# Lightning attention before a snake MLP: the product with the state in 64x64 tiles of four quadrants, in two passes

## The chip, the cores and the metric

One Trainium2 chip, one NeuronCore of it, one launch. The metric is the device time of the launch in microseconds. The kernel before took 213.11 us (median of 3 runs, 212.89 to 213.43). Engines are named as in the profile: PE is TensorE (its sequencer PEq), PEld its weight loads, DVE is VectorE, ACT is ScalarE, POOL is GpSimd, SP is SyncE, which here only issues DMAs.

## The reference, cut to what matters

Batch 4, 8 heads, 768 positions, head size 64; the attention goes in blocks of 64 positions with a running state of 64x64 a head. Its output, 3072 rows of 512, feeds an MLP with 2048 hidden columns.

```python
for b in range(nb):                                   # 12 blocks of 64 positions
    intra = einsum('bhic,bhjc->bhij', qb, kb) * Dmask # local scores, masked by decay
    intra = einsum('bhij,bhjd->bhid', intra, vb)
    inter = einsum('bhid,bhde->bhie', qb * lam_pow, kv_state)   # the product with the state
    out[:, :, sl] = intra + inter
    kv_state = lam_block * kv_state + einsum('bhsd,bhse->bhde', kb * rev_pow, vb)
h = x @ w_in                                          # x: out with the heads side by side
s = sin(alpha * h)
g = h + s * s / alpha
return g @ w_out
```

## The kernel before, in words

**Chunks and groups.** The 768 positions are cut into six chunks t of 128. A chunk of all four batches makes 512 rows of x, kept transposed in `xt[t]` (four blocks of 128 columns of the model, 512 rows), which is also a group g of the MLP. Everything is ordered by hand: the kernel's Python code writes the instructions in the order in which each engine runs them.

**The MLP.** A group has sixteen slots f. `hidden(g, f)` (L398) is four matmuls of 512 columns into a PSUM bank, then a sine on ScalarE (L405) and a square, on ScalarE (L408) or, for odd f of group 0, VectorE (L416). `finish(g, f)` (L413) on VectorE makes the column block of `gall` from the square and the bank, and so frees the bank. From group 1's fourth slot on, three banks go round, so `hidden(g, f)` needs `finish(g, f-3)`. `project(g, m, part)` (L422) is four matmuls of 512 columns, a quarter of an output tile; such units stand in a list `behind`, and `run(1)` takes the next. A unit with part 3 is followed by a copy out of PSUM (L434 on VectorE, L436 on ScalarE) and a store through SP. In slots that have a larger attention stage, `run` is skipped (L628).

**The attention of chunk g+1** is laid into the slots of group g. For chunks 2 to 5, in blocks of 64: `states` (L328, matmuls L331) makes the blocks' k-v products, `update` (L335 and `new_state` L306) adds them on VectorE to the decayed state (L313, four instructions for a pair of batches and a block) and GpSimd casts the state to BF16 into `SBD` (L317); `scores` (L342, matmuls L350) and `masks` (L354) make the masked local scores; `outputs` (L361) makes the product with the state (L368) and the local product (L376) into four banks, one for each pair of batches and block; `leave` (L382) scales the banks on VectorE into `xt`. Banks 4 to 7 serve states, scores and outputs one after the other. `slots(g)` (L582) puts states, scores and outputs into slots 7, 10 and 12 of group 1 and 4, 8 and 12 of the later groups. `feed(g)` (L599) places the loads of the next chunks (`pair_load`), the transposes of k and q by DMA (`turn_by_dma`, issued by SP) and GpSimd's decay of k (`pair_ready`).

Chunks 0 and 1 go in one block of 128 by `turns` (L227, transposes on TensorE, evicted by ScalarE), `scores1` (L268) and `outs` (L279, with the product with the state in L283 and the local one in L287), `states1` (L296). Chunk 0 is the prologue; chunk 1's transposes and scores stand in slots 12 to 15 of group 0 and behind it (L545 to L579).

**The product with the state.** Partitions hold two heads (hp, hd): head 2 hp in the lower 64, head 2 hp + 1 in the upper. `SBD` holds, for each batch and pair of heads, a 128x128 weight with the two 64x64 states on the diagonal and zeros beside them, so that one matmul over 128 rows gives both heads; x's blocks of 128 columns hold heads 2c and 2c+1. The zeros are written once: one buffer by VectorE (L146), two by GpSimd (L512). Each cast (L317) writes 64 partitions, so there are two of them for each update.

**Loads.** `load` (L101), `load_w_in` (L88, L93) and `load_w_out` (L96) are DMAs issued by GpSimd, in its program order between its own work. Eight can be in flight: each waits for the landing of the eighth before it.

Of the kernel before, what the change touches and what calls it, by code (L numbers as in the profile page):

```python
# [15 lines left out]
def kernel(  # L16
# [70 lines left out]
    def load_w_in(i):  # L87
        nc.gpsimd.dma_start(out=w_in_sb[i][:],  # L88
                            in_=moe_w_in[:, i * 512:(i + 1) * 512].rearrange("(c p) g -> p c g", p=P))

    def load_w_in0(n):
        w = slice(256 * n, 256 * n + 256)
        nc.gpsimd.dma_start(out=w_in_sb[0][:, :, w], in_=moe_w_in[:, w].rearrange("(c p) g -> p c g", p=P))  # L93
# [22 lines left out]
    load_w_in0(0)  # L116
    load_w_in0(1)
# [26 lines left out]
    SBD = [consts.tile([P, B, HP, 2, D], BF16, name=f"sbd{n}") for n in range(3)]  # L144
    S_of = [consts.tile([P, B, HP, D], FP32, name=f"S{n}") for n in range(2)]
    nc.vector.memset(SBD[1][:], 0.0)  # L146
# [12 lines left out]
    ln_hd = consts.tile([P, HP], FP32, name="ln_hd")  # L159
    for hd, half in enumerate(HALF):  # L160
        nc.vector.tensor_copy(out=ln_hd[half, :], in_=by_pair[half, hd, :])
# [8 lines left out]
    def decay_tables():  # L170
        later["R128"] = powers("R128", 2, lnlam[:], [P, H])
        later["NE64"] = powers("NE64", 3, by_pair, [P, 2, HP])
        later["R64"] = powers("R64", 4, lnlam[:], [P, H])
        nc.scalar.activation(out=L128[:], in_=ln_hd[:], func=ACTF.Exp, scale=float(T))
        nc.scalar.activation(out=L64[:], in_=ln_hd[:], func=ACTF.Exp, scale=float(D))

    def etab(*hps):
        for hp in hps:
            nc.scalar.activation(out=Etab[:, hp, :], in_=pos_row[:], func=ACTF.Exp, scale=ln_hd[:, hp:hp + 1])
# [15 lines left out]
    def home(t, blk):  # L195
        return SBD[2 if blk else t % 2]

# [80 lines left out]

    def outs(t, b, n, eng=None):  # L279
        O = bank("O_ps", n)[:].rearrange("p (c i) -> p c i", c=HP)  # L280
        if t:
            for hp in range(HP):
                nc.tensor.matmul(out=O[:, hp, :], lhsT=home(t, 0)[:, b, hp, :, :], rhs=QT[t][:, b, hp, :],  # L283
                                 start=(hp == 0), stop=False, skip_group_check=True)
        for hp in range(HP):
            for hd in range(2):
                nc.tensor.matmul(out=O[halves(hd), hp, :], lhsT=vn[t][:, b, 2 * hp + hd, :],  # L287
                                 rhs=STm[t, b][:, hd, hp, :], start=(t == 0 and hp == 0), stop=True,
# [17 lines left out]
    def new_state(n, pr, ps, decay, dst):  # L306
# [9 lines left out]
        for hd in range(2):  # L316
            nc.gpsimd.tensor_copy(out=dst[halves(hd), bs, :, hd, :], in_=S[halves(hd), bs, :, :])  # L317
# [42 lines left out]

    def outputs(t):  # L361
        O = {(pr, blk): bank("O_ps", AB[2 * pr + blk])[:].rearrange("p (u c i) -> p u c i", u=2, c=HP)
             for pr in range(2) for blk in range(2)}
        for pr in range(2):
            for blk in range(2):
                for u in range(2):
                    for hp in range(HP):
                        nc.tensor.matmul(out=O[pr, blk][:, u, hp, :], lhsT=home(t, blk)[:, 2 * pr + u, hp, :, :],  # L368
                                         rhs=QT[t][:, 2 * pr + u, hp, halves(blk)],
                                         start=(u == 0 and hp == 0), stop=False, skip_group_check=True)  # L370
        for pr in range(2):
            for u in range(2):
                for hp in range(HP):
                    for blk in range(2):
                        for hd in range(2):
                            nc.tensor.matmul(out=O[pr, blk][halves(hd), u, hp, :],  # L376
# [302 lines left out]
```

## Time and profile before

| | us |
|---|---|
| median of 3 runs (lowest, highest) | 213.11 (212.89, 213.43) |
| the profiled execution, in all | 213.7 |
| its span, first to last instruction | 211.9 |
| PE busy, matmuls | 201.8 |
| DVE busy | 136.6 |
| ACT busy | 141.4 |
| POOL busy | 99.4 |

How to read it: the span is one profiled execution's time from the first to the last instruction; the profiled execution as a whole took 1.8 us longer, for what lies around it. "Busy" is the time in which an engine had at least one instruction of its own running; matmuls overlap, so a matmul's duration is longer than the distance to the next. The distance of two starts in the timeline says what a group of matmuls costs TensorE. In a timeline row the first number is the start in us from the span's start, the second the length, then engine, line, operation, names and count; in brackets how long the engine stood idle before it and what ended that. In rows of groups, "x16 | 10.3, 684" is the count, the busy us and the mean ns of one. The granted clock of TensorE was 1.0 throughout.

### The profile page before, as it was taken

The numbers are of one execution on the slowest core, as the hardware profiler recorded it, in microseconds if no ns is written. First come the engines' busy times: TensorE is split into PE (matmuls) and PEld (weight loads), VectorE is DVE, ScalarE is ACT, GpSimd is POOL, SyncE is SP. The second block draws the span as 40 slices with busy tenths as digits, with TensorE's granted clock in tenths as the row PEclk, the third lists the DMA queues.
The fourth block names the chain that finished last, engine by engine and source line by source line (L and its number), as shares of the span: only waits on it lengthen the run. The fifth ranks groups of instructions, "written<-read, shape, count | busy, mean of one in ns | idle before, by whom it ended". The sixth has DMA issues, their size and how long they took to land.

```text
span 211.9 us, 4823 instructions
## 1 busy us (share of the span) xinstructions
PE 201.8 (95%) x1961; PEld 100.0 (47%) x1961; DVE 136.6 (64%) x258; ACT 141.4 (67%) x229; POOL 99.4 (47%) x104
## 2 busy tenths in 40 slices
PE   6679998999998999999999999999999999999993
PEld 2444444654444644446444446444446444444452
DVE  5675995774589888987649977648767544444000
ACT  4695988506895698764776765776774787887121
POOL 8999979985499995999003930004000000000000
PEclk9999999999999999999999999999999999999999
DMA  5999999999999999999999007711101101110212
GB/s 104 154 161 206 206 161 182 182 180 155 166 219 180 128 138 148 183 146 120 182 146 200 37 20 104 150 46 53 53 0 53 49 0 49 49 52 2 99 52 98
DMA packets 98759, 24.44 MB, mean 115 GB/s; under 512 B 90913, under 2 KB 95793, under 8 KB 98737
## 3 DMA queue, kind: packets, MB, share of 16 engines
q0 software_dynamic: 77040, 13.37, 85.0%
q1 hardware_dynamic: 20512, 10.50, 24.5%
q10 hardware_dynamic: 1184, 0.27, 0.6%
q8 instruction: 15, 0.25, 0.5%
q14 instruction: 8, 0.06, 0.1%
HBM read 27.28 MB, written 6.29 MB: 158 GB/s over the span
## 4 chain that ended last, share of the span: by engine, by line
PE 70%; DMA 10%; DVE 7%; ACT 5%; issue 3%; POOL 3%; DVEq 0%; ACTq 0%; POOLq 0%
PE ops L427 34%; PE hps L402 26%; DMA qn<-in_q_dram 10%; DVE S L313 4%; ACT s_sb L405 3%; DVE gall L417 2%; PE O_ps L368 2%; ACT s L408 2%; PE hps L445 2%; POOL kn L101 1%; PE F_ps L350 1%; PE O_ps L376 1%; PE KV_ps L331 1%; POOL kdec L208 1%; PE O_ps L287 1%
## 5 line engine op out<-in xcount | busy, mean ns | idle before, releaser
L417 DVE SCALAR_TENSOR_TENSOR gall<-s,r_sb,hps 128x512 bf16<-128x512 bf16 x96 | 71.0, 744 | 44.6 <-ACT s L408 44.3
L402 PE MATMUL hps<-xt,w_in 128*128 128x512 bf16 x384 | 96.4, 379 | 0.6 <-DVE xt L294 0.3
L405 ACT ACTIVATE s_sb<-hps,alpha_sb 128x512 bf16<-128x512 f32 x96 | 65.5, 685 | 47.0 <-PE hps L402 47.0
L427 PE MATMUL ops<-w_out,gall 128*128 128x512 bf16 x368 | 92.5, 379 | 0.0
L408 ACT ACTIVATE s<-s_sb 128x512 bf16<-128x512 bf16 x90 | 56.7, 630 | 2.9
L402 PEld LDWEIGHTS <-w_in 128*128 128x128 bf16 x384 | 36.8, 98 | 45.2 <-issue 1.8
L427 PEld LDWEIGHTS <-gall 128*128 128x128 bf16 x368 | 34.6, 98 | 40.4 <-issue 0.6
L317 POOL CAST sbd<-S 64x512 bf16<-64x512 f32 x36 | 22.0, 611 | 44.6 <-DVE S L313 40.8
L208 POOL TENSOR_TENSOR kdec<-kn,R 128x1024 bf16<-128x1024 bf16 x12 | 22.7, 1899 | 1.8 <-DMA kn<-in_k_dram 1.2
L313 DVE SCALAR_TENSOR_TENSOR S<-S,L,KV_ps 128x128 f32<-128x128 f32 x64 | 17.3, 342 | 0.0
L101 POOL DMA_DIRECT2D kn<-in_k_dram x13 | 14.8, 1138 | 0.3 <-issue 0.3
L101 POOL DMA_DIRECT2D qn<-in_q_dram x13 | 14.3, 1097 | 0.0
L101 POOL DMA_DIRECT2D vn<-in_v_dram x12 | 14.0, 1170 | 0.2 <-issue 0.2
L384 DVE TENSOR_TENSOR xt<-O_ps,Etab 128x512 bf16<-128x512 f32 x16 | 10.3, 684 | 3.4 <-PE O_ps L376 3.4
L436 ACT COPY o_sb<-ops 128x512 f32<-128x512 f32 x11 | 6.3, 573 | 8.3 <-PE ops L427 8.3
L276 DVE TENSOR_TENSOR STm<-F_ps,C 128x512 bf16<-128x512 f32 x16 | 10.1, 683 | 1.9 <-PE O_ps L287 1.1
L434 DVE COPY o_sb<-ops 128x512 f32<-128x512 f32 x12 | 8.3, 691 | 4.3 <-PE ops L427 4.3
L357 DVE TENSOR_TENSOR STm<-F_ps,C 128x512 bf16<-128x512 f32 x16 | 10.2, 682 | 0.0
L456 PE MATMUL hps<-fill 128*128 128x256 bf16 (+1 forms) x32 | 7.6, 361 | 1.5 <-DVE fill L122 1.5
L249 ACT COPY QKT<-T_ps 128x512 bf16<-128x512 bf16 x8 | 4.5, 585 | 1.9 <-PE T_ps L247 1.9
L294 DVE TENSOR_TENSOR xt<-O_ps,Etab 128x512 bf16<-128x512 f32 x7 | 4.6, 683 | 1.1 <-PE O_ps L287 1.1
L368 PEld LDWEIGHTS <-sbd 128*128 128x128 bf16 x128 | 4.3, 98 | 0.9
(73 smaller groups left out, 95.5 us busy)
## 6 DMA issues: line engine op xcount, KB each, us to landing
out_dram<-o_sb SPq DMA_DIRECT2D x23, 256.0 KB, 2.3
vn<-in_v_dram POOLq DMA_DIRECT2D x12, 256.0 KB, 13.2
kn<-in_k_dram POOLq DMA_DIRECT2D x10, 256.0 KB, 10.4
qn<-in_q_dram POOLq DMA_DIRECT2D x10, 256.0 KB, 12.3
w_out<-in_moe_w_out_dram POOLq DMA_DIRECT2D x4, 512.0 KB, 15.4
w_in<-in_moe_w_in_dram POOLq DMA_DIRECT2D x3, 512.0 KB, 12.2
w_in<-in_moe_w_in_dram POOLq DMA_DIRECT2D x2, 256.0 KB, 8.0
kn<-in_k_dram POOLq DMA_DIRECT2D x3, 128.0 KB, 5.8
```

The lines of the kernel that those rows point to most:

```text
L101: nc.gpsimd.dma_start(out=dst[t][:, b0:b1, :, :].rearrange("p b h e -> p (b h) e"), in_=src[b0:b1, :, t * T:(t + 1) * T, :].rearrange("b h ...
L208: nc.gpsimd.tensor_tensor(out=kdec[t][:, b0:b1, :, :], in0=kn[t][:, b0:b1, :, :], in1=R[:].unsqueeze(1).unsqueeze(3).broadcast_to([P, b1 - ...
L276: nc.vector.tensor_tensor(out=st[:, hd], in0=Fb[hd], in1=C0[:, hd], op=ALU.mult)
L313: nc.vector.scalar_tensor_tensor(out=S[:, bs, hp, :], in0=old[:, bs, hp, :], scalar=decay[:, hp:hp + 1], in1=ps[:, :, hp, :], op0=ALU.mult ...
L317: nc.gpsimd.tensor_copy(out=dst[halves(hd), bs, :, hd, :], in_=S[halves(hd), bs, :, :])
L357: nc.vector.tensor_tensor(out=st[:, hd], in0=att["F"][pr, hd], in1=C64[:, hd].unsqueeze(1).broadcast_to([P, 2, HP, D]), op=ALU.mult)
L384: nc.vector.tensor_tensor(out=xview(t)[:, 2 * pr:2 * pr + 2, blk, :, :], in0=att["O"][pr, blk], in1=Eb, op=ALU.mult)
L402: nc.tensor.matmul(out=hps[:], lhsT=w[:, c, (f % 4) * P:(f % 4 + 1) * P], rhs=xt[g][:, c, :], start=(c == 0), stop=(c == NDC - 1))
L405: nc.scalar.activation(out=s_sb[:], in_=hps[:], func=ACTF.Sin, scale=alpha_sb[:, f:f + 1])
L408: nc.scalar.activation(out=s2[:], in_=s_sb[:], func=ACTF.Square)
L417: nc.vector.scalar_tensor_tensor(out=gall[g][:, f, :], in0=s2[:], scalar=r_sb[:, f:f + 1], in1=hps[:], op0=ALU.mult, op1=ALU.add)
L427: nc.tensor.matmul(out=ops[:], lhsT=gall[g][:, f, m * P:(m + 1) * P], rhs=w_out_sb[part][:, f % 4, :], start=(f == 0), stop=(f == NFC - 1))
```

## The change

The state's buffers `SB` hold only the states (half the size, no zeros), and the product goes in matmuls of 64 rows and 64 columns, one for each head, batch and block, each in one of the four quadrants of the array: the row half is that of the head's place in q and the state, the column half that of its place in x. So that both halves of columns are used, x's block c now holds heads c (lower 64) and c + 4 (upper 64); w_in's rows are loaded to match, in two halves of 64 partitions each (ten DMAs for five), and the table `Etab` of decays is laid out likewise (`ln_x`).

Matmuls of the two row halves write the same bank only in different passes. The first ("crossed") pass and the second are kept apart by a fence: a tiny copy in place of a few elements of the transposed q, which has to wait for the first pass and which the second pass's first matmul waits for. Chunk 1 does this for a pair of batches (`pair_inter`, fence on ScalarE); chunks 2 to 5 for all four batches (`outputs_crossed`, fence on GpSimd), with hidden 12 of the later groups, and hidden 13 of group 1, between the passes.

Moved besides: in group 0, chunk 1's transposes go by pair (k of batches 0 and 1 in slot 12, q in slot 13), a unit goes into slot 15, and the stages behind the group are reordered around the passes, with other banks; in group 1, chunk 2's `states` go from slot 7 to 6, the transposes of q from 6 to 5, the decay of k from 4 to 3, chunk 3's loads from slots 7 and 8 to 6 and 7, and `outputs` from 12 to 13 with the crossed pass in 12. The slots without a `run` stay. The fills with zeros go; a cast writes 128 partitions; two decay tables are made by four activations in place of two.

```diff
-    def load_w_in(i):
-        nc.gpsimd.dma_start(out=w_in_sb[i][:],
-                            in_=moe_w_in[:, i * 512:(i + 1) * 512].rearrange("(c p) g -> p c g", p=P))
...
+    def load_w_in(i, w0=0, w1=512):
+        for n, half in enumerate(HALF):
+            nc.gpsimd.dma_start(
+                out=w_in_sb[i][half, :, w0:w1],
+                in_=moe_w_in[n * NDC * D:(n + 1) * NDC * D, i * 512 + w0:i * 512 + w1].rearrange(
+                    "(c e) g -> e c g", e=D))
...
-    SBD = [consts.tile([P, B, HP, 2, D], BF16, name=f"sbd{n}") for n in range(3)]
+    SB = [consts.tile([P, B, HP, D], BF16, name=f"sb{n}") for n in range(3)]
...
-    nc.vector.memset(SBD[1][:], 0.0)
...
+    ORDER = ([(hp, hd) for hp in (0, 2, 1, 3) for hd in (0, 1)], [(hp, hd) for hp in (3, 1, 2, 0) for hd in (1, 0)])
+
+    def fence(eng, ap):
+        if eng is nc.scalar:
+            eng.copy(out=ap, in_=ap)
+        else:
+            eng.tensor_copy(out=ap, in_=ap)
...
+    def pair_inter(t, pr, second, ns=()):
+        for u, n in enumerate(ns):
+            O_of[t, 2 * pr + u] = bank("O_ps", n)[:].rearrange("p (c i) -> p c i", c=NDC)
+        for hp, hd in ORDER[second]:
+            b, h = 2 * pr + (hd ^ second), 2 * hp + hd
+            nc.tensor.matmul(out=O_of[t, b][halves(h // NDC), h % NDC, :],
+                             lhsT=home(t, 0)[halves(hd), b, hp, :], rhs=QT[t][halves(hd), b, hp, :],
+                             start=(not second and hp in (0, 2)), stop=False, skip_group_check=True)
+        if not second:
+            fence(A, QT[t][HI, 2 * pr:2 * pr + 2, 3, 0:1])
...
-        for hd in range(2):
-            nc.gpsimd.tensor_copy(out=dst[halves(hd), bs, :, hd, :], in_=S[halves(hd), bs, :, :])
+        nc.gpsimd.tensor_copy(out=dst[:, bs], in_=S[:, bs])
...
+    def inter(t, pr, crossed):
+        for u in (0, 1) if crossed else (1, 0):
+            for hp, hd in ORDER[not crossed]:
+                b, h, blk = 2 * pr + u, 2 * hp + hd, hd ^ crossed
+                nc.tensor.matmul(out=att["O"][pr, blk][halves(h // NDC), u, h % NDC, :],
+                                 lhsT=home(t, blk)[halves(hd), b, hp, :],
+                                 rhs=QT[t][halves(hd), b, hp, halves(blk)],
+                                 start=(crossed and u == 0 and hp in (0, 2)), stop=False,
+                                 skip_group_check=True)
+
+    def outputs_crossed(t):
...
+        for pr in (1, 0):
+            inter(t, pr, True)
+        fence(G, QT[t][HI, 1, 3, 0:T:D])
+
     def outputs(t):
...
         for pr in range(2):
+            inter(t, pr, False)
             for u in range(2):
...
         if f == 12:
-            turns(1, 0, 6)
+            turns_pair(1, "k", 0, 6, (A, A))
         if f == 13:
-            turns(1, 1, 4)
+            turns_pair(1, "q", 0, 4, (A, A))
...
         if f == 15:
             scores1(1, 1, (4, 5))
-            outs(1, 0, 6)
+            run(1)
         finish(0, f)
     pair_load(2, 0)
+    pair_inter(1, 0, False, (6, 2))
+    turns_pair(1, "k", 2, 4, (A, A))
+    pair_inter(1, 0, True)
+    outs(1, 0, 6)
     run(1)
-    turns_pair(1, "k", 2, 2, (A, A))
-    outs(1, 1, 4)
-    run(1)
+    outs(1, 1, 2)
     turns_pair(1, "q", 2, 6, (A, V))
...
     run(1)
-    scores1(1, 2, (5, 2))
-    scores1(1, 3, (4, 6))
+    scores1(1, 2, (5, 4))
+    scores1(1, 3, (2, 6))
     decay_k(1, 2, 4)
     pair_load(2, 1)
-    run(2)
+    run(1)
+    pair_inter(1, 1, False, (5, 4))
+    run(1)
+    pair_inter(1, 1, True)
     outs(1, 2, 5)
     run(1)
-    outs(1, 3, 6)
+    outs(1, 3, 4)
     run(1)
...
         if g == 1:
-            at = dict(KV=7, F=10, O=12)
+            at = dict(KV=6, F=10, O=13)
...
+        if g == 1:
+            d[at["O"] - 1] += [(outputs_crossed, t)]
...
-            d[4] += [(pair_ready, 2, 1)]
+            d[3] += [(pair_ready, 2, 1)]
             d[4] += [(turn_by_dma, 2, 1, "k")]
-            d[6] += [(turns_pair, 2, "q", 2, 5, (V, V))]
+            d[5] += [(turns_pair, 2, "q", 2, 5, (V, V))]
...
-                d[7] += [(new_chunk, 3), (pair_load, 3, 0)]
-                d[8] += [(pair_load, 3, 1)]
+                d[6] += [(new_chunk, 3), (pair_load, 3, 0)]
+                d[7] += [(pair_load, 3, 1)]
...
+            if g > 1 and g + 1 < NT and i == 12:
+                outputs_crossed(g + 1)
             if g < NT:
                 hidden(g, i)
```

68 lines of the change are left out of this document (29 added, 39 removed).

## The prediction

> **What bounds the kernel now.** I read the page first, then the timeline of TensorE, then that of VectorE and ScalarE around the stages that the diff touches, then the DMA issues. Below, hidden 12 is the hidden stage with f = 12 of its group, a unit is four project matmuls (L427), and times count from the span's start.
>
> ```profile
> span 211.9 us, 4823 instructions
> PE 201.8 (95%) x1961; PEld 100.0 (47%) x1961; DVE 136.6 (64%) x258; ACT 141.4 (67%) x229; POOL 99.4 (47%) x104
> L405 ACT ACTIVATE s_sb<-hps,alpha_sb 128x512 bf16<-128x512 f32 x96 | 65.5, 685 | 47.0 <-PE hps L402 47.0
> L408 ACT ACTIVATE s<-s_sb 128x512 bf16<-128x512 bf16 x90 | 56.7, 630 | 2.9
> ```
>
> ScalarE mostly waits for TensorE (47.0 us on L402). So a microsecond off TensorE's row is a microsecond off the end, unless TensorE then stands waiting for somebody else. The next view, TensorE's timeline, says what the product with the state (L368) costs in chunks 2 to 5; chunk 3:
>
> ```profile
> 88.70 1.02 PE L402 MATMUL hps<-xt,w_in 128*128 128x512 bf16 x4
> 89.65 0.74 PE L350 MATMUL F_ps<-QKT 64*64 64x64 bf16 x64
> ...
> 96.37 1.03 PE L402 MATMUL hps<-xt,w_in 128*128 128x512 bf16 x4
> 97.24 1.10 PE L368 MATMUL O_ps<-QKT,sbd 128*128 128x64 bf16 x32
> 98.26 0.74 PE L376 MATMUL O_ps<-STm,vn 64*64 64x64 bf16 x64
> 98.93 1.04 PE L427 MATMUL ops<-w_out,gall 128*128 128x512 bf16 x4
> ...
> 143.88 0.69 PE L331 MATMUL KV_ps<-vn,kdec 64*64 64x64 bf16 x32
> 144.51 1.04 PE L427 MATMUL ops<-w_out,gall 128*128 128x512 bf16 x4
> ```
>
> Read the differences of the starts. L368 holds TensorE 1.02 us, L376 0.67 us. Four hidden matmuls take 0.87 us (96.37 to 97.24), but 0.95 us (88.70 to 89.65) where 64*64 tiles follow: a change of tile size costs some 0.09 us. 64 matmuls in four quadrants take 0.67 us and 32 in two quadrants 0.63 us: the time goes by sets, and four tiles work at once. Within L376, 63 starts lie in 0.74 - 0.19 = 0.55 us, 8.7 ns each (0.19 is one matmul's own length); the way out takes 0.67 - 0.55 = 0.12 us.
>
> **Chunks 2 to 5.** 32 matmuls become 64 of a quarter. Crossed pass: 0.09 + 31 x 8.7 ns + 0.12 = 0.48 us. Second pass and local product together, 96 matmuls: 0.09 + 95 x 8.7 ns + 0.12 = 1.04 us. 1.52 against 1.69 us: **-0.17 us a chunk**. That is all that "no zeros" brings, since the split adds two changes of tile size. The wait that it adds is GpSimd's tiny copy between the passes. Between them stand four hidden matmuls and two changes, 0.87 + 0.17 = 1.04 us. Bounds for a copy that no row shows: nothing, and the 0.61 us of the cast below; with the 0.19 us of the last matmul and two hand-overs of some 0.05 us it is back after at most 0.9 us. I take no wait. Behind the copy on GpSimd's queue stand kdec and the loads of the next-but-one chunk, which now can't run ahead of it; kdec is needed eight slots later, the loads after that.
>
> ```profile
> L317 POOL CAST sbd<-S 64x512 bf16<-64x512 f32 x36 | 22.0, 611 | 44.6 <-DVE S L313 40.8
> ...
> w_in<-in_moe_w_in_dram POOLq DMA_DIRECT2D x3, 512.0 KB, 12.2
> ```
>
> ```profile
> L88 POOL DMA_DIRECT2D w_in<-in_moe_w_in_dram x3 | 2.3, 800 | 0.0
> ```
>
> **Start and loads.** The casts become half as many (one of 128 partitions for two of 64), the fills with zeros go from VectorE and GpSimd, ScalarE gets two more tiny activations: GpSimd is idle 44.6 us ahead of its casts, and the other two engines have slack there; I cost them at nothing. The order of x's blocks costs nothing either: the same rows of w_in are loaded elsewhere. w_in's five loads become ten, so GpSimd issues for up to 5 x 0.8 = 4 us longer, less the fills that went behind them, and with eight loads in flight it waits now and then for a landing before kdec. But the order of bytes in the DMA queue stays, and a load of w_in waits 12.2 us to land: 4 us later into a backlog of 12 is not later out of it. Bounds: 0, and +4 us if nothing were backlogged; I take 0, the nearer row being the 12.2. Of the loads that chunk 2's moved stages carry, those of chunk 3 go out a slot earlier behind fewer casts; SP's queue keeps its order.
>
> **Chunk 1 (the head).**
>
> ```profile
> 31.45 0.39 PE L233 MATMUL T_ps<-iden,kn 128*128 128x128 bf16 x4
> 31.51 0.63 ACT L408 ACTIVATE s<-s_sb 128x512 bf16<-128x512 bf16 x1
> ...
> 32.32 0.40 PE L233 MATMUL T_ps<-iden,qn 128*128 128x128 bf16 x4 [0.48 <-DMA qn<-in_q_dram]
> 32.55 1.03 PE L402 MATMUL hps<-xt,w_in 128*128 128x512 bf16 x4
> ...
> 34.82 0.40 PE L272 MATMUL F_ps<-QKT 64*128 64x128 bf16 x8
> 35.15 1.04 PE L402 MATMUL hps<-xt,w_in 128*128 128x512 bf16 x4
> 35.72 1.28 DVE L276 TENSOR_TENSOR STm<-F_ps,C 128x512 bf16<-128x512 f32 x2
> ...
> 37.05 0.38 PE L283 MATMUL O_ps<-QKT,sbd 128*128 128x128 bf16 x4 [0.22 <-DVE STm L276]
> 37.37 0.41 PE L287 MATMUL O_ps<-STm,vn 128*64 128x128 bf16 x8
> 37.71 1.04 PE L427 MATMUL ops<-w_out,gall 128*128 128x512 bf16 x4
> ...
> 39.23 1.07 ACT L264 COPY QKT<-T_ps 128x512 bf16<-128x512 bf16 x2 [0.82 <-PE T_ps L261]
> ...
> 47.45 1.03 PE L402 MATMUL hps<-xt,w_in 128*128 128x512 bf16 x4
> ```
>
> Now q's transposes wait for q at 32.32. After, k's eight run from 31.45 (0.23 us for four, 0.45 for eight), hidden 13 until 32.76, and only then q's, which has landed: that wait goes. But ScalarE is a queue: square 12 ends 31.51 + 0.63 = 32.14, two k copies 1.07, sine and square 13 (0.69 + 0.63), and the first q copy ends at 34.93. The scores of batch 0 start at 34.97 where they started at 34.82; TensorE waits there 0.8 us instead. Then scores 0.33, hidden 15 and a change 0.96, scores 0.33, a project unit 0.87, first pass from 37.55. In 64*64 tiles with 128 columns no row exists; between 0.03 us a set (the 64-column rows) and 0.12 us (two quadrants at a time; 37.05 to 37.37 has 0.32 us for four full matmuls and a change) I take 0.06, a pass of two sets with its changes 0.32 us. k's next transposes need bank 4 from the first mask of batch 1; VectorE does that mask (half of 1.28 us) behind the finish of 14, which follows square 14 (36.67), and has it at 38.03: 0.25 us of waiting. The fence runs on ScalarE behind square 15 (37.9) and is hidden by these transposes. Transposes, second pass, two outs (0.35 each), one unit: q's transposes at 40.50, as now (40.57). From there the same work with two passes more against eight L283, a wait of 0.14 us for batch 2's masks and three changes of tile size: hidden(1,0) at **47.69 instead of 47.45, +0.24 us**.
>
> **Group 1, where chunk 2's stages moved.**
>
> ```profile
> 60.17 1.02 PE L331 MATMUL KV_ps<-vn,kdec 64*64 64x64 bf16 x64
> 61.12 1.04 PE L402 MATMUL hps<-xt,w_in 128*128 128x512 bf16 x4
> ...
> 65.55 0.47 PE L350 MATMUL F_ps<-QKT 64*64 64x64 bf16 x33
> 66.39 0.38 PE L350 MATMUL F_ps<-QKT 64*64 64x64 bf16 x22 [0.38 <-DVE S L313]
> 67.15 0.26 PE L350 MATMUL F_ps<-QKT 64*64 64x64 bf16 x9 [0.38 <-issue]
> 67.34 1.04 PE L427 MATMUL ops<-w_out,gall 128*128 128x512 bf16 x4
> ...
> 76.17 1.89 PE L402 MATMUL hps<-xt,w_in 128*128 128x512 bf16 x8
> ```
>
> ```profile
> 61.47 2.15 DVE L313 SCALAR_TENSOR_TENSOR S<-S,L,KV_ps 128x128 f32<-128x128 f32 x8
> 63.53 0.74 DVE L417 SCALAR_TENSOR_TENSOR gall<-s,r_sb,hps 128x512 bf16<-128x512 bf16 x1
> 64.19 2.15 DVE L313 SCALAR_TENSOR_TENSOR S<-S,L,KV_ps 128x128 f32<-128x128 f32 x8
> ...
> 74.19 1.28 DVE L384 TENSOR_TENSOR xt<-O_ps,Etab 128x512 bf16<-128x512 f32 x2
> ```
>
> The scores take 1.79 us instead of 0.67: one wait for VectorE's update, one that the profile puts down to nothing. States and updates a slot earlier end the first. States start at 60.17 - 0.87 + 0.24 = 59.55. But VectorE is full here, and a hidden stage needs the bank that the finish three slots before frees. VectorE's queue after: hidden 5 starts at 56.88 (59.55 less a change, two hidden stages and a unit), its product, sine and square take 1.07 + 0.69 + 0.66, so finish 5 (0.67 as 63.53 to 64.19) runs behind q's copies until 60.07; update 2.15 (62.2), finish 6 (62.86), update (64.93), finish 7 (65.59). TensorE: states until 60.22, hidden 7, 8, a unit, hidden 9 at 62.91, a unit until 64.64, then hidden 10 **waits 1.0 us** for finish 7: 65.64. Scores 66.60 to 67.27, against 67.34 now. The wait has only changed its place. On: crossed pass 70.83, outputs 72.17 to 73.10 (a slot later than before), hidden 14, 15 and a unit until 75.69. hidden(2,0) needs the last of leave: hidden 12 starts at 69.87, so finish 12 runs from 72.30 to 73.05 by the same three times; then leave (1.2), finish 13 (0.67) and leave until 76.10, so 76.15 against 76.17. The head's loss is repaid, and chunk 2's gain spent on VectorE.
>
> **The sum.** -0.02 at 76.15, some -0.03 up to chunk 3's states, 3 x -0.17: -0.56 us on the span of 211.9, so 211.3; the profiled execution took 213.7 in all, 0.6 over the median of the runs (213.11). 213.11 - 0.56 = **212.5**.
>
> **Rivals.**
> *VectorE is not so late* (0.25): if finish 7 comes a microsecond sooner than my queue has it (it decides from 64.6 down), hidden 10 doesn't wait, the waits of 1.1 us in the scores are gained, outputs and leave follow earlier by as much, and hidden(2,0) stands at 75.2: another -1.0, 211.5. For it: the second wait in the scores has no owner and may just go, and a finish placed ahead of an update would do. Against it: VectorE's queue as written above.
> *Chunk 2's v lands late* (0.2, slower). States a slot earlier need batches 2 and 3 of v.
>
> ```profile
> 45.95 1.16 POOL L101 DMA_DIRECT2D vn<-in_v_dram  x1
> ```
>
> ```profile
> DMA to landing us min/median/max: 6.7/13.2/15.6
> ```
>
> Issued at 45.95, it lands at 59.2 by the median of vn's loads and at 61.6 by the longest; it is needed at 59.85. Past that each microsecond goes into VectorE's chain and so to hidden(2,0): by the longest +1.7, 214.2; half of that, 213.4.
> *The fence is late* (0.05, slower): each 0.1 us past 1.04 costs 0.4 us in four chunks; a copy of twice the cast's 0.61 us is back after 1.5 us, +0.47 x 4, 214.4. Against it: GpSimd's queue is then empty by the order of its instructions.
> *The quadrants run two at a time* (0.05, the change doesn't do what it says): 64 matmuls at 16.1 ns (L331 at 143.88: 0.69 - 0.19 over 31 starts) cost 64 x 7.4 ns = 0.47 us more a chunk and 8 x 0.06 in chunk 1: 212.5 + 1.9 + 0.5 = 214.9. Against it: L350 and L376, 8.7 ns. [...]
>
> **How the numbers follow.** My forecast has 0.45, its own range 211.9 to 213.1. Faster by over 0.3% (0.64 us, about what a measurement of this kernel can tell from no change) is below 212.47: the first rival and half the forecast, 0.47. Within: the rest of the forecast and a third of v's case, 0.30. Slower, above 213.75: two thirds of v's case and the last two, 0.23. The range that leaves out 2 in 10 goes from 211.3 to 214.0.
>
> **What would show it.** Right: 32 + 96 matmuls in 0.48 and 1.04 us with changes; no wait ahead of the second pass in chunks 2 to 5; hidden(1,0) near 47.7; hidden 10 of group 1 waiting for gall L444 (the finish) and unbroken scores behind it; hidden(2,0) near 76.1 waiting for the leave. Wrong: a wait for GpSimd, states waiting for v, 16 ns a quadrant matmul, or hidden 10 not waiting.

## The result

The changed kernel took **217.15 us** (median of 4 runs, 215.18 to 218.62) against 213.15 for the kernel before on the same chip (212.89 to 213.43); ratio 1.0146, 95% interval 1.0099 to 1.0193. Three runs (218.62 here, 219.73 and 217.17 below) were disturbed as a whole and are in no ratio. By the ratio the change costs 3.1 us (2.1 to 4.1). The prediction was 212.5 with a range to 214.0: wrong in sign. The profiled execution is the quickest of the four (215.18), and its span is only 1.5 us longer than that of the kernel before; the rest has to be found by experiment.

The head of the page of the changed kernel, and its row of TensorE's instruction queue:

```profile
span 213.4 us, 5113 instructions
PE 201.4 (94%) x2105; PEld 97.3 (46%) x2105; DVE 137.3 (64%) x257; ACT 142.8 (67%) x235; POOL 88.6 (42%) x93
...
q8 instruction: 16, 0.26, 0.5%
```

TensorE is as busy as before (201.4 against 201.8 us), in a span 1.5 us longer: it waits more. The last row is a DMA queue for instructions, sixteen packets of 16 KB. That they are TensorE's follows from their count: 15 packets beside 3946 records of TensorE in the kernel before, 16 beside 4238 here, 17 beside 4340 in the first experiment, one for every 256 records behind the first 193. TensorE's timeline says where it waits. Chunk 3, to be held against the rows at 96.37 to 98.93 of the kernel before:

```profile
97.18 1.03 PE L454 MATMUL ops<-w_out,gall 128*128 128x512 bf16 x4
98.13 0.45 PE L383 MATMUL O_ps<-QKT,sb 64*64 64x64 bf16 x32
98.51 1.04 PE L429 MATMUL hps<-xt,w_in 128*128 128x512 bf16 x4
99.48 0.32 PE L383 MATMUL O_ps<-QKT,sb 64*64 64x64 bf16 x16
99.62 0.46 PE L404 MATMUL O_ps<-STm,vn 64*64 64x64 bf16 x32
99.89 0.33 PE L383 MATMUL O_ps<-QKT,sb 64*64 64x64 bf16 x16
100.04 0.61 PE L404 MATMUL O_ps<-STm,vn 64*64 64x64 bf16 x32
100.58 1.04 PE L454 MATMUL ops<-w_out,gall 128*128 128x512 bf16 x4
```

The crossed pass takes 0.38 us, the second with the local product 1.10; with the two changes of tile size ahead of them (0.95 and 0.97 us for what is 0.86 otherwise) 1.67, where the kernel before took 1.69. Read the starts of the second: 16 matmuls in 0.14 to 0.15 us, 32 in 0.27, the last 32 in 0.54. Some 0.12 of the 0.54 is the change of tile size on the way out; the 31 starts within the last row still take 0.61 - 0.19 = 0.42 us, 13.5 ns a matmul for 8.7. The pace falls towards the end. No row waits for GpSimd: the fence is free (its copy takes 0.19 us, from 98.83 on, and the second pass starts at 99.48). And four quadrants do work at once: 31 starts of the crossed pass in 0.45 - 0.19 = 0.26 us, 8.4 ns a matmul, where 32 matmuls in two quadrants took 16.1 in the kernel before.

Group 1, the head's rows and the moved stages of chunk 2:

```profile
35.41 0.40 PE L271 MATMUL F_ps<-QKT 64*128 64x128 bf16 x8 [0.71 <-ACT QKT L263]
...
38.53 0.61 PE L260 MATMUL T_ps<-iden,kn 128*128 128x128 bf16 x8 [0.22 <-DVE STm L275]
...
48.13 1.03 PE L429 MATMUL hps<-xt,w_in 128*128 128x512 bf16 x4
```

```profile
59.99 0.74 PE L349 MATMUL KV_ps<-vn,kdec 64*64 64x64 bf16 x64
...
66.13 1.02 PE L429 MATMUL hps<-xt,w_in 128*128 128x512 bf16 x4 [0.84 <-DVE gall L444]
67.08 0.74 PE L368 MATMUL F_ps<-QKT 64*64 64x64 bf16 x64
...
72.66 0.32 PE L383 MATMUL O_ps<-QKT,sb 64*64 64x64 bf16 x16
72.80 0.46 PE L404 MATMUL O_ps<-STm,vn 64*64 64x64 bf16 x32
73.10 0.19 PE L383 MATMUL O_ps<-QKT,sb 64*64 64x64 bf16 x1
74.72 0.32 PE L383 MATMUL O_ps<-QKT,sb 64*64 64x64 bf16 x15 [1.43 <-issue]
...
77.84 1.46 PE L429 MATMUL hps<-xt,w_in 128*128 128x512 bf16 x6
```

The waits that the prediction placed are there: the scores of batch 0 for ScalarE's copies, k's transposes for the mask, hidden 10 for the finish, unbroken scores. One is there that it did not place: between two matmuls of the same line, inside one burst (from 73.10 to 74.72), TensorE stands 1.6 us, and the profile names nobody ("issue"). Counting TensorE's records (matmuls, weight loads and its 28 semaphore waits and drains) from the trace's start, it stands after number 1473. The kernel before stands in its scores after number 1217 (the `<-issue` that the prediction quotes at 67.15, 0.38 us of idle time and 0.57 us lost from start to start): 256 fewer. And in the trace's DMA records a packet of the instruction queue starts at 72.31, 2.41 us ahead of the matmul at 74.72; in the kernel before at 64.61, 2.54 us ahead of the one at 67.15. The DMA view of the window from 72.2 to 72.4 us shows it among full queues (packets, MB, share of 16 engines):

```profile
q1 hardware_dynamic: 80, 0.02, 77.1%
q0 software_dynamic: 80, 0.01, 76.8%
q8 instruction: 1, 0.02, 29.6%
```

**Theory 1.** TensorE's instructions come in blocks of 256 (the sixteen packets of 16 KB, and the two waits 256 records apart). The next one is asked for when the last is begun: that is the theory's assumption, for in the traces the packet of 72.31 starts 4.9 us after that and the one of 64.61 4.1. It is there 2.2 to 2.9 us after its packet starts (2.41 and 2.54 above; the range is that of eight traces). The change makes 64 matmuls of 32 (each with a weight load), so chunk 2's scores and outputs use up 256 instructions in 5.7 us, and TensorE runs dry. How many blocks TensorE holds no run here shows. **Theory 2**, about the runs that are slower still: the ten loads of w_in, which keep GpSimd from its own work until VectorE needs its time too. **Rivals**: the wait belongs to the place (GpSimd, a DMA, contention), whatever its number in the stream; or the moved stages cost the time.

### The profile page after: what moved, and what is told of

It is laid out like the page before. It is cut to its first block, busy times and chain, and to the rows that moved or that the text cites. A ratio compares the mean times of both kernels' runs of the same rounds, so it can differ in the third digit from the quotient of the medians.

```text
span 213.4 us, 5113 instructions
## 1 busy us (share of the span) xinstructions
PE 201.4 (94%) x2105; PEld 97.3 (46%) x2105; DVE 137.3 (64%) x257; ACT 142.8 (67%) x235; POOL 88.6 (42%) x93
## 4 chain that ended last, share of the span: by engine, by line
PE 72%; DVE 13%; ACT 5%; DMA 4%; POOL 3%; issue 2%; DVEq 0%; POOLq 0%; ACTq 0%
PE ops L454 34%; PE hps L429 28%; DVE gall L444 6%; DVE S L332 4%; DMA vn<-in_v_dram 4%; ACT s_sb L432 3%; ACT s L435 2%; PE hps L472 2%; PE O_ps L383 2%; POOL kn L100 1%; DVE s L443 1%; PE F_ps L368 1%; POOL qn L100 1%; PE O_ps L404 1%; PE KV_ps L349 1%
## 5 line engine op out<-in xcount | busy, mean ns | idle before, releaser
L335 POOL CAST sb<-S 128x512 bf16<-128x512 f32 x18 | 11.0, 621 | 31.5 <-DVE S L332 31.5
L285 POOL COPY QKT<-QKT 64x2 bf16<-64x2 bf16 x4 | 0.8, 191 | 32.9 <-PE O_ps L383 20.5
L89 POOL DMA_DIRECT2D w_in<-in_moe_w_in_dram x10 | 6.2, 660 | 2.4 <-DMA vn<-in_v_dram 2.4
```

The costliest lines, as they stand in the source:

```text
L335: nc.gpsimd.tensor_copy(out=dst[:, bs], in_=S[:, bs])
```

## The experiments

All times are medians beside runs of the kernel before on the same chip; times of the kernel before are 213.05 to 213.25. Six edits add tiny matmuls that compute nothing, only to move the grid of 256:

```python
def nudge(n):
    ps = bank("hps", 1)          # or another free bank
    for i in range(n):
        nc.tensor.matmul(out=ps[HALF[i % 2], 0:16], lhsT=fill[LO, 0:D], rhs=fill[LO, 0:16], start=True, stop=True)
```

### Moving the grid in the start-up

```diff
-    spin(9, 0, 512)
+    spin(8, 0, 512)       # 7 for a shift of 160 or 176
+    nudge(52)             # 80: shift of 160; 88, in the kernel before: shift of 176
```

> The kernel after with 52 tiny matmuls (104 instructions of TensorE) in the start-up, where TensorE only spins, one spin fewer: the same work later, but each block of 256 instructions begins 104 instructions earlier in the program. Theory (TensorE's instructions come in blocks of 256, each asked for when the block before is begun and there some 7 us later while DMA is busy; the 1.6 us stall of chunk 2's second pass is a late block): the two blocks around chunk 2's scores and outputs now take 9 and 7.7 us of work instead of 5.7, so the stall at 73.1 us is gone and no new one comes; span 211.7 to 212.2, time 213.3 to 214.0, and less spread from run to run. Rival (the stall belongs to the place: GpSimd, a DMA or contention there, whatever the position in the program): stall unchanged, time 215 to 218 as the kernel after.

> The kernel after with 80 tiny matmuls (160 instructions) in the start-up, two spins fewer. Theory: a block begins just ahead of chunk 2's crossed pass and the next one just inside the end of its local product, some 2.2 us of work apart, so the stall there grows to 4 to 5 us, its place the last matmuls of L404 of chunk 2: span 216 to 217.5, time 218 to 219.5. Rival (the stall belongs to the place): unchanged at 1.6 us in L383, time 215 to 218, no difference from a shift of 104 instructions.

> The kernel before with 88 tiny matmuls (176 instructions) in the start-up, two spins fewer. Theory: the ownerless wait of 0.5 us in chunk 2's scores (67.15 us) is the same late block; with the grid shifted by 176 no block is used up faster than in 7.4 us, the wait goes, and since VectorE's leave ends that stretch part of the gain is lost to a later wait: time 212.5 to 213.1. Rival: unchanged, the wait stays in the scores, 213.1.

Measured: 217.19 (216.86 to 217.53), 217.94 (217.47 to 218.20) and, for the kernel before with a shift, 213.70 (213.15 to 215.22; ratio 1.0036, 1.0011 to 1.0062). As times all three missed, and that of shift 104 lies where the rival had it. The traces decide for theory 1. Shift 104, chunk 2's second pass:

```profile
75.54 0.32 PE L383 MATMUL O_ps<-QKT,sb 64*64 64x64 bf16 x16
75.69 0.46 PE L404 MATMUL O_ps<-STm,vn 64*64 64x64 bf16 x32
75.95 0.36 PE L383 MATMUL O_ps<-QKT,sb 64*64 64x64 bf16 x16
76.11 0.54 PE L404 MATMUL O_ps<-STm,vn 64*64 64x64 bf16 x32
76.58 1.90 PE L429 MATMUL hps<-xt,w_in 128*128 128x512 bf16 x8
```

Unbroken. Shift 160, the hidden stage behind that pass:

```profile
77.04 0.82 PE L429 MATMUL hps<-xt,w_in 128*128 128x512 bf16 x3
78.35 1.24 PE L429 MATMUL hps<-xt,w_in 128*128 128x512 bf16 x5 [0.49 <-issue]
```

The ownerless wait has gone to another line, after record 1729 (1473 + 256), with a packet at 75.62, 2.73 us ahead. It is 0.65 us (0.87 from start to start for 0.22) instead of 4 to 5, since here the packet started within about a microsecond of the block's beginning instead of 4.9: the fixed delay that theory 1 was given is wrong. In the kernel before with a shift of 176 the scores wait for VectorE only:

```profile
66.95 0.44 PE L350 MATMUL F_ps<-QKT 64*64 64x64 bf16 x31 [0.39 <-DVE S L313]
```

(x22 and x9 with a wait between them before.) Why the times missed: the shift brought a block's fetch into the start-up, among chunk 0's loads. With 104 it starts at 12.02 us, q's last load landed at 11.94 as ever (11.84), the next one, v, at 14.84 instead of 13.64. So one packet of 16 KB goes with a slip of 1.2 us of the loads behind it, and hidden(0,0) moves from 17.62 to 18.99. The other two shifts show the same: with a packet at 9.48 and at 9.67 us, q's last load lands at 13.00 instead of 11.84, and k's last at 12.43 instead of 10.83. And a second thing showed, in group 0 of shift 104 and only slightly in the profiled execution of the change (squares of 0.42, 0.64 and 0.65 us): VectorE's and GpSimd's rows.

```profile
21.43 0.75 DVE L444 SCALAR_TENSOR_TENSOR gall<-s,r_sb,hps 128x512 bf16<-128x512 bf16 x1 [2.59 <-ACT s L435]
22.10 2.02 DVE L443 TENSOR_TENSOR s<-s_sb 128x512 bf16<-128x512 bf16 x1
...
25.48 0.89 DVE L443 TENSOR_TENSOR s<-s_sb 128x512 bf16<-128x512 bf16 x1
```

```profile
22.98 1.17 POOL L100 DMA_DIRECT2D qn<-in_q_dram  x1
24.14 1.93 POOL L207 TENSOR_TENSOR kdec<-kn,R 128x1024 bf16<-128x1024 bf16 x1
```

```profile
28.98 0.44 PE L321 MATMUL KV_ps<-vn,kdec 128*64 128x64 bf16 x16 [0.72 <-DVE gall L444]
29.35 1.04 PE L429 MATMUL hps<-xt,w_in 128*128 128x512 bf16 x4
31.35 1.02 PE L429 MATMUL hps<-xt,w_in 128*128 128x512 bf16 x4 [0.96 <-DVE gall L444]
```

A square on VectorE (L443) that takes 0.42 us elsewhere takes 2.02, until GpSimd's kdec starts, and 0.89 within kdec; TensorE then waits 1.7 us for `gall` in group 0. In the kernel before this doesn't happen: its kdec run at 13.7 and 17.9 us, before the first square at 20.4. The changed kernel issues ten loads of w_in, has eight in flight (the seventh of the ten goes out at 13.92 us, behind the landing of the eighth load before it, v's first, at 13.64, the next one at 15.90, behind v's second at 15.61), and reaches kdec at 18.5.

### The passes cut 64 and 64

Abridged; `local` is the local product of a pair of batches, `inter` its product with the state:

```diff
-        for pr in (1, 0):
-            inter(t, pr, crossed)
+        local(t, 0); inter(t, 1, crossed); inter(t, 0, uncrossed)        # first pass
...
-        for pr in range(2):
-            inter(t, pr, uncrossed); local(t, pr)
+        inter(t, 0, crossed); inter(t, 1, uncrossed); local(t, 1)        # second pass
```

> The kernel after with the passes of chunks 2 to 5 cut otherwise: first pass = local product and uncrossed product of batches 0 and 1 with the crossed one of batches 2 and 3 (64 matmuls), second pass the rest (64 matmuls), instead of 32 and 96. Same matmuls, same changes of tile size. Theory (past some 64 matmuls without a long one, TensorE's instructions come at half the pace, which ate the 0.17 us a chunk): both passes take 0.67 us from start to next start where 32 and 96 take 0.38 and 1.10, so 0.14 us less in each of chunks 3 to 5; in chunk 2 the stall of 1.6 us stays within 0.3 us, since the block still begins at the same instruction. Time 0.4 to 0.6 us under the kernel after. Rival (the loss is a fixed cost of the second fence and the tile changes): the sum of both passes unchanged at 1.47 us.

216.72 (215.27 to 219.73; ratio 1.0151, 1.0111 to 1.0191): no difference that these runs can show, and its trace is that of its longest run. The trace of kernel c below, which has this cut too, does show one. In its chunk 4, against the 0.38 + 1.10 us of the changed kernel in chunk 3:

```profile
128.00 0.44 PE L393 MATMUL O_ps<-STm,vn 64*64 64x64 bf16 x32
128.27 0.43 PE L382 MATMUL O_ps<-QKT,sb 64*64 64x64 bf16 x32
128.64 1.04 PE L431 MATMUL hps<-xt,w_in 128*128 128x512 bf16 x3
129.61 0.45 PE L382 MATMUL O_ps<-QKT,sb 64*64 64x64 bf16 x32
129.88 0.51 PE L393 MATMUL O_ps<-STm,vn 64*64 64x64 bf16 x32
130.33 1.04 PE L456 MATMUL ops<-w_out,gall 128*128 128x512 bf16 x3
```

0.64 + 0.72: 0.12 us less a chunk, with the same fence and the same changes of tile size. So the slow pace goes with the length of the burst, not with the second fence; yet the second 64 still take 0.08 us more than the first, and why stays open.

The changed kernel slows after some 130 to 150 instructions (from 4.3 to 6.8 ns an instruction, each matmul with its weight load), and kernel c within its second 64 matmuls: no one count of instructions in a burst fits both, and what limits the pace the runs don't show.

In chunk 2 of the kernel of this experiment the ownerless wait again stood after record 1473, though that is now the 17th matmul of the second pass instead of the 49th: position, not place. It was 3.1 us there, in the longest run, and not the 1.6 us expected.

### The loads of w_in and kdec

Abridged:

```diff
 # the kernel before, ten half loads
-        nc.gpsimd.dma_start(out=w_in_sb[i][:], in_=moe_w_in[...].rearrange("(c p) g -> p c g", p=P))
+        for half in HALF:
+            nc.gpsimd.dma_start(out=w_in_sb[i][half], in_=moe_w_in[...].rearrange("(c p) g -> p c g", p=P)[half])
 # the changed kernel, five whole loads: load_w_in as in the kernel before
 # the changed kernel, kdec between the loads
-    load_w_in(1); load_w_in(2); load_w_in(3); load_w_out(0); decay_k(0, 0, 2)
+    load_w_in(1); decay_k(0, 0, 2); load_w_in(2); decay_k(0, 2, 4); load_w_in(3); load_w_out(0)
 # the changed kernel, the shift by 104 behind v's landing
-    spin(2, 6)
+    nudge(52)
     outs(0, 2, 2)
```

> The kernel before with w_in's five loads cut into ten of 64 partitions (same rows, old order of x's blocks), nothing else. Theory (GpSimd, with ten loads to issue and eight in flight, reaches kdec and chunk 1's loads some 4 us later, and these then run while VectorE makes the squares of group 0; a square takes 0.42 us alone and up to 2 us beside GpSimd's work): kdec starts at about 18.5 us instead of 13.7, some squares of group 0 take 0.6 to 2.0 us, hidden stages of group 0 wait up to 2 us for gall; time 213.6 to 216 and a spread over 1 us. Rival (the ten loads cost nothing beyond the landing of the first, as the prediction had it): squares at 0.42 us, time 213.1 to 213.5 with before's spread of 0.5 us.

> The kernel after with w_in in five whole loads as before. The rows of w_in are then in the old order while x's blocks hold heads c and c+4, so the product h = x w_in mixes rows; sizes and work are the same. Theory: kdec back at 13.7 us, all squares of group 0 at 0.42 us, hidden(0,0) within 0.15 us of 17.25, spread down to some 1 us; the stall for TensorE's instructions in chunk 2 stays: 214.0 to 215.5. Rival (the ten loads are not the cause of the spread): 215 to 218 as the kernel after.

> The kernel after with GpSimd's order changed: the two kdec of chunk 0 stand between the loads of w_in, where GpSimd waits 1 and 1.4 us for a landing anyway, instead of behind all ten. Theory (kdec and the issues beside VectorE's squares): kdec at 14 to 19 us; the squares of group 0 back to 0.42 us or stretched by less than 0.3 us, no wait for gall in group 0; 214.3 to 215.5 with the instruction stall of chunk 2 left in. Rival: the issue of chunk 1's loads, still at 20 to 24 us, holds the squares by itself: squares of 1 to 2 us stay, time 215 to 218.

> The kernel after with the same 52 tiny matmuls as in the shift by 104, but behind the landing of chunk 0's first two batches of v, in place of two spins, where TensorE waits 1 us anyway; so no block of instructions is fetched among chunk 0's loads (that fetch moved v by 1.2 us there). Theory: chunk 2's stall is gone and hidden(0,0) starts within 0.2 us of 17.6; what is left of the loss is group 0: 213.5 to 216. Rival (the late start of the shifted kernel came from the tiny matmuls themselves): hidden(0,0) at 18.5 or later.

- **Ten half loads alone make the kernel before slower by 1.5 us**: 214.71 (213.53 to 214.81), ratio 1.0068 (1.0051 to 1.0085). Its profiled execution is the quickest one (213.53), so the trace holds only 0.3 of it: kdec at 18.53 us, two stretched squares, v landing at 15.60 us instead of 15.19 and hidden(0,0) at 17.61 instead of 17.25:

```profile
22.59 0.58 DVE L414 TENSOR_TENSOR s<-s_sb 128x512 bf16<-128x512 bf16 x1
...
24.58 0.63 DVE L414 TENSOR_TENSOR s<-s_sb 128x512 bf16<-128x512 bf16 x1
```

- **Five whole loads in the changed kernel** (sizes and work are the same, but x and the rows of w_in no longer match): 214.20 (213.62 to 217.17; ratio 1.0041, 1.0027 to 1.0056), squares of 0.42 us, v landing at 15.35, hidden(0,0) at 17.44. Against the 1.0146 of the change that is 2.2 us less, and the intervals lie apart.
- **kdec between the loads**: 215.66 (215.18 to 215.98; ratio 1.0112, 1.0091 to 1.0133). By the ratio that is 0.7 us less than the change, with intervals that overlap: these runs can't tell it from nothing. The runs spread over 0.8 us instead of 2.8 (three runs of the change). v still lands at 15.76. All six squares are back:

```profile
20.88 0.42 DVE L442 TENSOR_TENSOR s<-s_sb 128x512 bf16<-128x512 bf16 x1
...
22.70 0.42 DVE L442 TENSOR_TENSOR s<-s_sb 128x512 bf16<-128x512 bf16 x1
...
24.51 0.42 DVE L442 TENSOR_TENSOR s<-s_sb 128x512 bf16<-128x512 bf16 x1
```

The loads of chunk 1 are issued in the same time (20.8 to 28.5 us), so their issue alone holds no square: the rival given with that run falls. What the traces show is that a square that overlaps kdec's row is stretched from 0.42 us to 0.58 to 0.89; beside the fill with zeros, in the kernel before with ten loads (GpSimd writes from 26.83 to 30.4 us), the squares at 27.17 and 29.55 take 0.42. Why the one holds a square and the other doesn't, they don't show. What held the 2.02 us square ahead of kdec's own row stays open; rows on GpSimd are rough.

The fourth kernel (52 tiny matmuls behind v's landing, in place of two spins) took 215.72 (214.99 to 215.77; 1.0109), within what was expected: chunk 2's ownerless wait gone, squares of 1.10 and 0.68 us, 0.62 us of waiting for `gall`. With no packet among the first loads, v landed at 13.81. But its start was late by another way, much as the rival had it: behind the tiny matmuls TensorE's next ones ran more slowly (eight of L306 in 0.64 us for 0.41), and hidden(0,0) came at 18.4.

### Putting the repairs together, and the moved stages alone

```diff
 a: kdec between the loads, and ahead of chunk 1's first scores (TensorE waits 0.7 us there):
+            nudge(52)
 b: a, and in slot 7 of group 1
+            finish(g, 7)      # ahead of update(t, 1) instead of behind it
 c: b, and the passes cut 64 and 64
 d: the kernel before with states, q's transposes, kdec and chunk 3's loads a slot earlier
-            at = dict(KV=7, F=10, O=12)
+            at = dict(KV=6, F=10, O=12)
+            finish(g, 7)      # ahead of update(t, 1)
```

> The kernel after with chunk 0's kdec between the loads of w_in (as tried alone, 215.66 us) and 52 tiny matmuls in group 0, ahead of chunk 1's first scores, where TensorE waits 0.8 us for ScalarE's copies anyway: the grid of 256 instructions moves by 104 from there on. Theory: no wait for gall in group 0 and no stall in chunk 2's second pass (1.5 us with kdec moved alone); up to 0.5 us of it comes back as a wait of hidden(2,0) for leave: 214.0 to 214.6. Rival (the stall belongs to the place): 215.2 to 216.

> As the kernel before it in this set, and in slot 7 of group 1 the finish of hidden 7 goes ahead of the second update in VectorE's queue. Theory (my own step of the prediction: hidden 10 waits 1 us because that finish stands behind the update): hidden 10 no longer waits, scores start some 0.9 us earlier just behind the update's end, and hidden(2,0) follows by 0.4 to 0.9 us: 213.2 to 214.0. Rival (VectorE's total in group 1 sets hidden(2,0) whatever the order): same as without.

> As the kernel before it in this set, with chunks 2 to 5's passes cut 64 and 64 instead of 32 and 96. Theory (half pace past some 64 small matmuls): 0.11 us less a chunk, as the two passes of chunk 3 showed in the kernel with that cut alone (0.64 + 0.72 us against 0.38 + 1.10): 0.3 to 0.5 us under the kernel before it. Rival: no difference.

> The kernel before, without the quadrants, but with chunk 2's states, transposes of q, decay of k and chunk 3's loads a slot earlier in group 1 as the change has them (outputs stay in slot 12), and the finish of hidden 7 ahead of the second update. It tells what the moved stages are worth without the quadrants. Theory: the two waits inside chunk 2's scores (0.4 us for VectorE's update; 0.5 us for instructions, which may move or stay) become one of at most 0.5 us, hidden(2,0) at 75.3 to 75.9 instead of 76.17: 212.3 to 213.0. Rival (moved stages cost: v late or VectorE fuller): 213.3 to 214.5.

| | us, median (range) | ratio (95% interval) |
|---|---|---|
| a | 215.22 (214.29 to 217.41) | 1.0114 (1.0054 to 1.0173) |
| b | 215.10 (214.57 to 216.03) | 1.0098 (1.0069 to 1.0127) |
| c | 214.49 (212.99 to 215.76) | 1.0067 (1.0038 to 1.0096) |
| d | 213.15 (212.36 to 214.69) | 1.0000 (0.9979 to 1.0022) |

In the traces of a, b and c no ownerless wait over 0.2 us is left in chunk 2, and none for `gall` in group 0: both causes are gone from the traces, and the times miss all the same. (The trace of a is that of its longest run: TensorE's start-up ran at two thirds of its pace up to some 17 us, and hidden(0,0) came at 20.5.) One reason is the next wait, as group 1 of c shows:

```profile
66.09 0.45 PE L367 MATMUL F_ps<-QKT 64*64 64x64 bf16 x32
67.54 0.45 PE L367 MATMUL F_ps<-QKT 64*64 64x64 bf16 x32 [1.00 <-DMA QKT<-kn]
...
73.36 0.51 PE L393 MATMUL O_ps<-STm,vn 64*64 64x64 bf16 x32
73.80 1.90 PE L431 MATMUL hps<-xt,w_in 128*128 128x512 bf16 x7
75.54 1.03 PE L456 MATMUL ops<-w_out,gall 128*128 128x512 bf16 x4
76.82 1.45 PE L431 MATMUL hps<-xt,w_in 128*128 128x512 bf16 x6 [0.25 <-DVE xt L413]
```

Hidden 10 no longer waits for the finish, as the step said; now chunk 2's second transposes of k by DMA land 1.0 us too late, and hidden(2,0) waits for VectorE's leave at 76.82, where the kernel before had it at 76.17. The moved stages alone (d) are worth nothing: there too the scores wait for these transposes (0.63 us), and another ownerless wait, of 0.4 us, stands behind the outputs, with a packet 2.44 us ahead.

### What delays a block, and two more places

```diff
 e: the kernel before, behind hidden 12 of group 0, where TensorE waits 0.5 us for q
+            nudge(16)
 f: the changed kernel with kdec between the loads;  g: c;  h: g and outputs in slot 12, crossed pass in 11
-                d[6] += [(new_chunk, 3), (pair_load, 3, 0)]
-                d[7] += [(pair_load, 3, 1)]
+                d[7] += [(new_chunk, 3), (pair_load, 3, 0)]
+                d[8] += [(pair_load, 3, 1)]
```

> The kernel before with 16 tiny matmuls (32 instructions, 0.26 us) in group 0 behind hidden 12, where TensorE waits 0.5 us for q anyway. Nothing else: no quadrants, no moved stage. Theory (blocks of 256 instructions): from there on the grid lies 32 instructions earlier; a block then begins in chunk 2's scores and the next in its local product, 5.3 us of work apart, while a block takes 6.6 to 7.3 us to come in that stretch: the ownerless wait leaves the scores and one of 1.3 to 2.0 us appears in L376 of chunk 2; hidden(2,0) some 1.2 us later than 76.17; time 213.9 to 214.8. Rival (the waits belong to the places in the after kernel's passes): no new wait, 213.1 to 213.5.

> The kernel after with chunk 0's kdec between the loads of w_in (tried alone: 215.66 us, stall of 1.5 us) and chunk 3's loads back in slots 7 and 8 of group 1. Theory A (the block is late because its one packet waits behind chunk 3's loads, which the change put a slot earlier): the block's fetch starts under 3.5 us after the block before it is begun instead of 4.8, the stall shrinks below 0.7 us, 214.6 to 215.0. Theory B (DMA is full there either way): stall 1.2 to 1.8 us, time as without.

> The kernel with all repairs (kdec between the loads, grid moved by 104, finish of hidden 7 ahead, passes 64 and 64: 214.49 us) with chunk 3's loads back in slots 7 and 8. Theory: chunk 2's second transposes of k, which landed at 67.5 us behind those loads and held the scores for 1.0 us, land about a microsecond sooner; the scores start at 66.2 to 66.5 unbroken and hidden(2,0) comes 0.3 to 0.8 us earlier: 213.7 to 214.3. Rival (the transposes are late because of their own source's landing): unchanged.

> As the kernel before it in this set, with chunk 2's outputs back in slot 12 and the crossed pass in 11. Theory (the outputs in slot 13 put leave behind hidden 13 and 14, which holds hidden(2,0)): outputs end about 0.9 us earlier unless the second mask holds the first pass by up to 0.7 us; hidden(2,0) at 75.5 to 76.3; 0.2 to 0.7 us under the kernel before it. Rival (VectorE's sum in group 1 sets hidden(2,0)): no difference.

- **e**: 213.32 (212.84 to 214.27; 1.0001, 0.9976 to 1.0027), the time of the rival. The ownerless wait left the scores. A block's edge still lies in them (at 67.6 us), but its packet had started 8.1 us ahead. The new wait did not come: the packet of the next block started 1.5 us after the block before it was begun, not 4.1. So a burst over a block's edge is needed, and a late packet as well.
- **f**: 215.63 (214.80 to 216.20; 1.0114). The packet starts 5.1 us after the block before is begun, the wait is 1.6 us: chunk 3's loads being a slot earlier is not what delays it. Theory A falls.
- **g**: 214.55 (213.81 to 216.71; 1.0080). The scores start at 66.56 unbroken and hidden(2,0) stands at 76.13, about as expected; the time misses, for now chunk 3's v is late, and its states wait 1.45 us:

```profile
83.47 0.45 PE L348 MATMUL KV_ps<-vn,kdec 64*64 64x64 bf16 x32 [1.45 <-DMA vn<-in_v_dram]
```

- **h**: 214.95 (214.39 to 216.60; 1.0073), a miss as well. The first pass waits 1.4 us for the second mask. Slot 12 is too early for it.

## Why the prediction was wrong

**The step that failed first is "I take 0, the nearer row being the 12.2" for the ten loads**, the costliest term. Measured: 1.5 us added to the kernel before by the ten loads alone, and 2.2 of the change's 3.1 us gone with five. The argument followed the bytes: 4 us later into a backlog of 12. They came hardly later: chunk 1's first k landed at 30.77 against 30.35. What came later was GpSimd's own work, kdec at 18.5 us instead of 13.7, into the squares of VectorE. With kdec put elsewhere the squares are whole again, but the 0.7 us that this brings is within the noise, so how much of the loss goes by the squares is not shown. The start was costed at nothing too: hidden(0,0) starts 0.4 us later, with v landing at 15.61 instead of 15.19. The ten loads alone give as much (17.61); five leave 0.2 of it, with two more activations ahead of the cast of xt.

**The step that failed next is the "-0.02 at 76.15" of the sum**, which gives every wait on the way an owner. The prediction saw the ownerless wait in the scores, and gave it to the first rival as one that "may just go". It was a late block of instructions, and the change, which doubles the instructions of the product, made 1.6 us of its 0.57 at the next block's edge. Shown: it moves with the count of instructions (records 1217, 1473, 1473 with the passes cut otherwise, 1729; after 1463 in four more traces, in which ten matmul records ahead of it are missing), is absent from that pass in all seven kernels with a shift of 104, and ends 2.2 to 2.9 us after a packet of the instruction queue in eight traces. Not settled: what sets the start of the packet. It comes 0.4 to 2 us after the block before is begun at some places, 4 to 5 at the one that counts, 24 near the end of the changed kernel, and once 0.9 us ahead of it by the count.

**-0.17 us a chunk** was -0.02. The first pass is right (0.47 for 0.48); the second with the local product is 1.20 with its change of tile size for 1.04, since 8.7 ns a matmul holds for 64 of them and not for 96.

**Right**: the head (+0.21 us from 31.92 to 48.13, for +0.24), with both waits and their owners; the states without a wait for v; hidden 10 waiting 1.0 us for the finish; unbroken scores; no wait for the fence; hidden(2,0) bound by leave, once the ownerless wait is gone (76.82 and 77.17 for 76.15; in the change itself it came at 77.84 and waited for nobody). The rivals on v, the fence and the quadrants did not come.

**The account.** The 1.5 us of the profiled execution lie 0.37 us in the start, 0.10 in group 0, 0.21 in the head and 0.99 in group 1, where the block's wait is 1.0 longer than before; some 0.2 is gained behind that, where the gain of the passes was to be 0.5. Of the 3.1 us of the ratio, 2.2 go with the ten loads, the start among them; 0.9 are left with five. The kernel c, which has the ten loads still but all of it repaired save the head and the start, is 1.3 us over the kernel before, and its runs spread over 2.8 us; the trace explains 0.65 of it (hidden(2,0)), the rest stays open. Whether the ten loads cost it in some other way is not tested: none of the repaired kernels was run with five. No version here beat the kernel before.

## What to carry to other kernels

Count instructions as well as time: where many small matmuls follow each other, ask when the last 256 (a block here) were used up, look for `<-issue` inside a burst, and move it with a few idle matmuls before explaining it otherwise. A load cut in two moves no more bytes, but it made the issuing engine 5 us later with its own work here: look which VectorE work that then meets. Where the profiled execution is the quickest of its runs, what the trace shows is a lower bound of the loss.

## What the runs showed of the hardware

TensorE's instructions came by DMA during the run, 256 to a packet of 16 KB (15 packets in the kernel before, 16 in the changed one); a packet took 0.9 to 1.6 us in these two kernels, where TensorE had to wait the block was usable 2.2 to 2.9 us after its packet's start, and with one of them among the first loads a load behind it landed 1.2 to 1.6 us later (three kernels). 64x64 matmuls in four quadrants went at 8.4 to 8.7 ns with their weight load for about 64 matmuls and at 13.5 ns after that. A VectorE square of 0.42 us took 0.58 to 0.89 beside GpSimd's product; in the kernels with a shift of 104 it took 2.02 just ahead of that product's row and 1.10 where it began 0.92 us ahead of it.
